# Keeping the third product's last tile on chip as the last stage's first tile, in a four-stage kernel on one core

## The chip, the core and the metric

The kernel runs on one core of a Trainium2 chip. The metric is the device time of one execution in microseconds (us). Three runs of the kernel before the change took 1687.85 to 1689.36 us, median 1688.62 us.

## What is computed

Attention in chunks of 64 over 8 batches of 8 heads, then a gated block (SwiGLU with a norm), then a block whose gate is `h * cos(h)`. Cut to what matters here:

```python
def _moe_ref(x, w_gate, w_val, w_out, rms_g):      # x: 4608 x 512, d_ff 1536
    ...
    return (silu * val @ w_out)

def _moe2_ref(x, w_in, w_out):                     # x: 4608 x 512, d_ff 2048
    h = x @ w_in
    g = h * np.cos(h)
    return (g @ w_out)
```

## The kernel before

Four stages follow each other, and TensorE (PE) does matmuls through all of them. Stage 1 does the attention and the two products with `w_gate` and `w_val`. Stage 2 multiplies by the first `w_out`. Stage 3 multiplies by `w_in` and applies the cosine gate. Stage 4 multiplies by the second `w_out` and stores the result. Stages 2 to 4 run over six tiles `s` of 768 tokens (`T`), each cut in two halves of 384 tokens (`H`, the block column `c`).

Each of these three products is made of 2 x 2 blocks `(r, c)` and of seven block products `j` in the place of eight: sums and differences of blocks are formed first (`operand`, `operand3`), then multiplied, and the seven results are combined. A block product `(s, j, g)`, called a product below, is 12 matmuls: two halves of the output by two chunks of the inner length by three, since every operand is split into a high and a low part. The high part is a cast on ScalarE (ACT) and the low part a subtraction on VectorE (DVE); both stand in `operand` (L249, L250) and every product needs both. The order of `j` is `PRODUCTS = (1, 7, 6, 2, 5, 4, 3)` in stage 4, with four groups `g` of features inside each `j`, so a tile is 28 products. In stage 4 product 1 needs the block (0, 0), product 7 the difference (1, 1) - (0, 1) in the buffer `tmp` (L235), product 6 two further differences (L238, L239), product 2 the block (1, 0), product 5 the changed (0, 1), product 4 another difference (L246), product 3 the block (1, 1). Operands are asked for `AHEAD = 5` products before their use. There is one buffer `tmp`.

Stage 3 ends every block with `turn`: for blocks (0, 0), (1, 1) and (0, 1) these are the sum `u` (L898, DVE), a cast to an integer (L906, ACT), a difference (L907, DVE), a sine (L908) and a square (L909, both ACT) and the last product (L910, DVE); block (1, 0) goes straight from PSUM through L912 (ACT), L913 and L914 (DVE), L915 (ACT) and L916 (DVE). The result stands in one of four buffers `r` and is stored to DRAM (`gd`, L919). In each group `g` the products 4 and 3 are put off into the next group (`tail`), so the last two products of stage 3 are 4 and 3 of group 3.

Stage 4 reads every block back from `gd`. For its first tile, tile 0, `early4` fetches a part of the blocks while stage 3 runs, for the six operands of `EARLY4`; the 14 other loads are issued at the start of stage 4 (L996 to L1003, issued through L820). Later tiles are fetched by `fetch4` once the products 4 and 3 have taken their operands of the tile ahead: two loads a group, each of both columns. All loads and stores stand in the one queue of SyncE (SP).

The weights of stage 4 (28 pieces of 512 KB, `w<-kout`, L158) take the places that stage 3's weights leave. The list `wanted` says which piece, or which early operand, takes the next place that `free` gives back. Five places are held back (`HELD`) to the start of stage 4.

The order of the instructions on PE is that of the code. That of ACT, DVE and SP in stages 3 and 4 is set by the framework's scheduler, which goes by its own estimate of when things are ready.

After the last matmul of the kernel, the last block is stored in two halves: one transposition (L981) and four stores each (L985).

Of the kernel before, what the change touches and what calls it, by code (L numbers as in the profile page):

```python
# [20 lines left out]
P = 128  # L21
# [11 lines left out]
SQ = 32  # L33
# [22 lines left out]
EARLY4 = 6  # L56
HELD = (2, 7, 5, 4, 3)
# [19 lines left out]
def kernel(  # L77
# [58 lines left out]
    wanted += last[:4] + [("op4", n, k) for n in range(EARLY4) for k in range(2)] + last[4:]  # L136
    place_of, weight, kept, early = {}, {}, {}, {}

    held = []

    def free(*tags):
        for tag in tags:
# [4 lines left out]
            if kind == "op4":  # L147
                continue
# [557 lines left out]
    made3 = [0]  # L706

    def fetch3(s):
        if s == 0:
            raw3[s] = {(r, c): early["x2", r, c] for r in range(2) for c in range(2)}  # L710
        elif s < NB:
            t = third_p.tile([P, 4, T], F32, tag="raw", name="rawx2", bufs=1)
            raw3[s] = blocks(t)
            c = s * T % PIECE
            nc.sync.dma_start(out=t, in_=x2d[s * T // PIECE][:, :, c : c + T])

    def operand3(s, j):
# [10 lines left out]
        pool = third_p if j in (1, 2, 6) else left_p  # L728
        o = pool.tile([P, 2, 2, H], F32R, tag="x3", name="x3", bufs=4)
        split(o, a, nc.vector)  # L730
# [79 lines left out]
    def fetch4(s, r, g):  # L810
        if s < NB:
            t = rw.tile([P, 2, T], F32, tag=f"raw{r}", name="rawg")
            raw4[s, g, r, 0], raw4[s, g, r, 1] = t[:, :, :H], t[:, :, H:]
            if s:
                load4(s, r, g, t, 0, T)
            return t

    def load4(s, r, g, t, lo, hi):
        c = s * T % PIECE
        nc.sync.dma_start(out=t[:, :, lo:hi], in_=gd[s * T // PIECE][:, g, 2 * r : 2 * r + 2, c + lo : c + hi])  # L820

    def operand4(s, j, g):
        n = made4[0]
        if n < EARLY4:
            tmp = third_p.tile([P, 2, H], F32, tag="tmp", name="tmp", bufs=1) if j == 7 else None
            to = [wp.tile([P, 2, H], F32R, tag=place_of["op4", n, k], name="xo") for k in range(2)]
            part = first4[g]
        else:
            tmp = tp.tile([P, 2, H], F32, tag="tmp", name="tmp") if j == 7 else None
            to = parts(xo_p)  # L830
            part = {(r, c): raw4[s, g, r, c] for r in range(2) for c in range(2)}
        ops4[s, j, g] = operand(j, part, tmp, lambda: to)
# [258 lines left out]
```

## Time and profile before

| | |
|---|---|
| runs, median (lowest to highest) | 1688.62 us (1687.85 to 1689.36) |
| profiled execution: its own time | 1687.49 us |
| profiled execution: span in the trace | 1685.7 us |
| PE busy | 1651.4 us, 98% |
| DVE busy | 1263.3 us, 75% |
| ACT busy | 860.2 us, 51% |
| HBM read, written | 183.24 MB, 125.30 MB |
| stage 4's first matmul | 1308.79 us |

The span runs from the first to the last instruction of the profiled execution; its own time is 1.79 us longer than that, for what lies around it. PE's busy time says little here, since matmuls are pipelined and their ends are modelled. What counts is how many matmuls go through in a stretch of time: in an undisturbed stretch all products take the same time, and a hold-up shows as fewer matmuls than that.

### The profile page before, as it was taken

To read this page: it belongs to the slowest core of one execution; us is meant where nothing else is said; L and a number is where in the kernel's file an instruction comes from. 1 tells how busy PE (TensorE), PEld (TensorE's weight loads), DVE (VectorE), ACT (ScalarE), POOL (GpSimd) and SP (SyncE) were. 2 spreads that over 40 slices of the span, in tenths; PEclk is the share of its full clock that TensorE was granted. 3 is DMA by queue.
4 is the path that set the end of the run, shared out by engine and by line. 5 is a ranking of instruction groups with operands and counts; after the bars stand their busy time and mean duration, and the time that the engine had idled before them with its cause. 6 is when DMAs were issued, how large, how long until landed. Compare 5 with 4: busy or idle time off the path is not lost.

```text
span 1685.7 us, 28029 instructions
## 1 busy us (share of the span) xinstructions
PE 1651.4 (98%) x11016; PEld 1535.1 (91%) x11016; DVE 1263.3 (75%) x1831; ACT 860.2 (51%) x1242; POOL 63.0 (4%) x104
## 2 busy tenths in 40 slices
PE   6999999999999999999999999999999899999998
PEld 5988888888888888999999999999999798999998
DVE  7974577787878741577777778888889668877885
ACT  4643344455444421344444488888888434434442
POOL 2321000000000000000000000000000000000000
PEclk9999999999999999999999999999999999999999
DMA  8523478788888828654445924324448962354331
GB/s 322 184 89 113 143 243 244 222 246 254 238 239 246 238 101 278 200 188 150 150 150 199 324 105 150 136 108 150 144 157 290 370 203 90 109 177 153 119 104 39
DMA packets 274661, 310.40 MB, mean 184 GB/s; under 512 B 83040, under 2 KB 218720, under 8 KB 274528
## 3 DMA queue, kind: packets, MB, share of 16 engines
q1 hardware_dynamic: 274528, 308.60, 55.7%
q8 instruction: 87, 1.43, 0.4%
q14 instruction: 46, 0.38, 0.1%
HBM read 183.24 MB, written 125.30 MB: 183 GB/s over the span
## 4 chain that ended last, share of the span: by engine, by line
PE 95%; DVE 3%; ACT 1%; DMA 1%; issue 1%; SPq 0%; POOL 0%; ACTq 0%; DVEq 0%
PE b L262 56%; PE v L262 18%; PE g L262 17%; PE o L453 1%; PE sc L359 1%; PE tr L429 1%; PE pt L397 1%; ACT xo L249 0%; DMA rawg<-gd 0%; DMA raw<-in_w_dram 0%; DVE rawg L239 0%; DVE xo L250 0%; DVE p L390 0%; DVE tmp L235 0%; DVE z L387 0%
## 5 line engine op out<-in xcount | busy, mean ns | idle before, releaser
L262 PE MATMUL b<-xo,w 128*128 128x384 f32 (+1 forms) x3576 | 621.6, 334 | 12.9 <-ACT xo L249 8.8
L262 PEld LDWEIGHTS b<-xo,w 128*128 128x128 f32 x3576 | 615.5, 188 | 18.9 <-ACT xo L249 12.0
L262 PE MATMUL b<-x,w 128*128 128x384 f32 x2016 | 351.8, 335 | 0.1
L262 PEld LDWEIGHTS b<-x,w 128*128 128x128 f32 x2016 | 349.0, 188 | 2.8 <-ACT z L893 2.1
L262 PE MATMUL v<-xt,w 128*128 128x512 f32 (+1 forms) x1416 | 321.7, 377 | 0.0
L262 PE MATMUL g<-xt,w 128*128 128x512 f32 (+1 forms) x1416 | 314.6, 372 | 0.0
L262 PEld LDWEIGHTS g<-xt,w 128*128 128x128 f32 x1416 | 250.0, 188 | 45.8
L262 PEld LDWEIGHTS v<-xt,w 128*128 128x128 f32 x1416 | 248.3, 190 | 44.9
L502 ACT ACTIVATE sg<-g 128x512 f32<-128x512 f32 (+1 forms) x118 | 66.1, 560 | 226.8 <-PE g L262 218.0
L249 ACT CAST xo<-rawg 128x768 fp32r<-128x768 f32 x140 | 114.8, 836 | 121.0 <-PE b L262 96.8
L250 DVE TENSOR_TENSOR xo<-rawg,xo 128x768 fp32r<-128x768 f32 x140 | 131.4, 953 | 51.6 <-ACT xo L249 51.3
L506 DVE TENSOR_TENSOR h<-sg,v 128x512 f32<-128x512 f32 (+1 forms) x100 | 67.5, 678 | 117.3 <-PE v L262 96.6
L249 ACT CAST xo<-rawh 128x768 fp32r<-128x768 f32 x102 | 81.6, 835 | 95.6 <-DMA rawh<-hd 49.2
L250 DVE TENSOR_TENSOR xo<-rawh,xo 128x768 fp32r<-128x768 f32 x102 | 93.0, 954 | 36.1 <-ACT xo L249 36.1
L910 DVE SCALAR_TENSOR_TENSOR r<-r,u 128x768 f32<-128x768 f32 x72 | 68.6, 953 | 21.5 <-ACT r L909 21.4
L908 ACT ACTIVATE r<-r 128x768 f32<-128x768 f32 x72 | 60.8, 845 | 33.3 <-DVE r L907 32.9
L907 DVE SCALAR_TENSOR_TENSOR r<-r,u 128x768 f32<-128x768 int32 x72 | 68.6, 953 | 11.1 <-ACT r L906 11.0
L898 DVE TENSOR_TENSOR u<-b,z 128x768 f32<-128x768 f32 x72 | 68.5, 952 | 7.9 <-ACT z L893 6.4
L249 ACT CAST xo<-tmp 128x768 fp32r<-128x768 f32 x42 | 35.2, 837 | 63.2 <-DVE tmp L235 62.6
L906 ACT CAST r<-u 128x768 int32<-128x768 f32 x72 | 59.7, 829 | 8.5 <-DVE u L898 8.5
L909 ACT ACTIVATE r<-r 128x768 f32<-128x768 f32 x72 | 60.9, 846 | 1.2
L893 ACT COPY z<-b 128x768 f32<-128x768 f32 x72 | 56.5, 793 | 7.1 <-PE b L262 5.2
(101 smaller groups left out, 1434.5 us busy)
## 6 DMA issues: line engine op xcount, KB each, us to landing
gd<-r SPq DMA_DIRECT2D x96, 384.0 KB, 2.5
rawg<-gd SPq DMA_DIRECT2D x42, 768.0 KB, 6.0
hd<-h SPq DMA_DIRECT2D x49, 512.0 KB, 4.6
kout<-wout SPq DMA_DIRECT2D x56, 448.0 KB, 4.7
w<-kout SPq DMA_DIRECT2D x49, 512.0 KB, 5.4
rawh<-hd SPq DMA_DIRECT2D x15, 1536.0 KB, 9.2
wraw<-in_w_dram SPq DMA_DIRECT2D x176, 128.0 KB, 3.2
qk<-in_qk_dram SPq DMA_DIRECT2D x36, 512.0 KB, 5.5
```

What stands on the lines that cost most here:

```text
L249: nc.scalar.copy(hi, a)
L250: nc.vector.tensor_tensor(lo, a, f32(hi), op=ALU.subtract)
L262: nc.tensor.matmul(acc, a, b, start=first and k == 0 and q == 0, stop=k == n - 1 and q == 2, skip_group_check=True)
L502: nc.scalar.activation(sg, g, AF.Silu)
L506: nc.vector.tensor_tensor(h, silu(acc[0]), acc[1], op=ALU.mult)
L893: nc.scalar.copy(t, acc)
L898: nc.vector.tensor_tensor(t, acc, part, op=ALU.add)
L906: nc.scalar.copy(k, u)
L907: nc.vector.scalar_tensor_tensor(q, k, -1.0, u, op0=ALU.mult, op1=ALU.add)
L908: nc.scalar.activation(q, q, AF.Sin, scale=math.pi)
L909: nc.scalar.activation(q, q, AF.Square, scale=math.sqrt(2 * PI2))
L910: nc.vector.scalar_tensor_tensor(q, q, -PI2, u, op0=ALU.add, op1=ALU.mult)
```

## The change

Stage 4 takes its tiles in the order 5, 0, 1, 2, 3, 4. `turn` leaves the 16 blocks of tile 5 in SBUF in the place of storing them: the blocks (0, c) in places of the weights (`z4` in `wanted`), the blocks (1, c) in tiles of their own (`quad`). Stage 4 uses them there as they are, and neither stores nor reads them. `early4`, `HELD` and the 14 loads at the start of stage 4 go. The places for early operands are now four pairs (`EARLY4 = 4`), for product 1 of tile 5.

Every block that is read back has a buffer of its own, named by its place (`q` + r, c, g): loads of 384 KB, one for each block, in the place of loads of 768 KB (stage 4) and of 1536 KB (stage 3's `fetch3`). Stage 3's ring of four result buffers becomes the four buffers of block (1, 1). A block is fetched as soon as its last reader is done: (0, 1) after product 5, (0, 0) and (1, 0) after product 4, (1, 1) after product 3. For tile 0 the blocks (0, c) are fetched at the end of stage 3.

Since 44 things now share 28 places, 16 of the 28 weight pieces of stage 4 come only when places get free in stage 4's first tile: 8 after its first four products, 4 after the operands of product 5, 4 after those of product 4.

The last transposition is cut in two (L984 to L986 of the changed kernel).

```diff
-EARLY4 = 6
-HELD = (2, 7, 5, 4, 3)
+EARLY4 = 4
...
-    wanted += last[:4] + [("op4", n, k) for n in range(EARLY4) for k in range(2)] + last[4:]
+    got = {c: [("z4", c, g) for g in range(4)] for c in range(2)}
+    op4 = [("op4", g, k) for g in range(EARLY4) for k in range(2)]
+    wanted += got[0][:1] + last[:4] + op4[:2] + got[1][:1] + got[0][1:2] + op4[2:4] + last[4:7]
+    wanted += got[1][1:2] + got[0][2:3] + op4[4:6] + last[7:10] + got[1][2:3] + op4[6:7] + got[0][3:]
+    wanted += op4[7:] + last[10:12] + got[1][3:] + last[12:]
...
+    def quad(r, c, k, dtype=F32):
+        pool = ring_p if (r, c) == (1, 1) else third_p
+        return pool.tile([P, 2, H], dtype, tag=f"q{r}{c}{k}", name="q")
...
-            t = third_p.tile([P, 4, T], F32, tag="raw", name="rawx2", bufs=1)
-            raw3[s] = blocks(t)
-            c = s * T % PIECE
-            nc.sync.dma_start(out=t, in_=x2d[s * T // PIECE][:, :, c : c + T])
+            raw3[s] = {(r, c): quad(1, 0, 2 * r + c) for r in range(2) for c in range(2)}
+            o = s * T % PIECE
+            for r in range(2):
+                for c in range(2):
+                    a = x2d[s * T // PIECE][:, 2 * r : 2 * r + 2, o + c * H : o + (c + 1) * H]
+                    nc.sync.dma_start(out=raw3[s][r, c], in_=a)
...
+    order4 = [NB - 1, *range(NB - 1)]
+    next4 = dict(zip(order4, order4[1:]))
+
+    def fetch4(s, r, c, g):
+        if s in next4:
+            s = next4[s]
+            raw4[s, g, r, c] = quad(r, c, g)
+            o = s * T % PIECE + c * H
+            nc.sync.dma_start(out=raw4[s, g, r, c], in_=gd[s * T // PIECE][:, g, 2 * r : 2 * r + 2, o : o + H])
 
     def operand4(s, j, g):
         n = made4[0]
+        tmp = third_p.tile([P, 2, H], F32, tag="tmp", name="tmp") if j == 7 else None
         if n < EARLY4:
-            tmp = third_p.tile([P, 2, H], F32, tag="tmp", name="tmp", bufs=1) if j == 7 else None
             to = [wp.tile([P, 2, H], F32R, tag=place_of["op4", n, k], name="xo") for k in range(2)]
-            part = first4[g]
         else:
-            tmp = tp.tile([P, 2, H], F32, tag="tmp", name="tmp") if j == 7 else None
             to = parts(xo_p)
-            part = {(r, c): raw4[s, g, r, c] for r in range(2) for c in range(2)}
...
+        ops4[s, j, g] = operand(j, {(r, c): raw4[s, g, r, c] for r in range(2) for c in range(2) if (s, g, r, c) in raw4}, tmp, lambda: to)
+        first = s == NB - 1
+        if j == 5:
+            if first:
+                free(place_of["z4", 1, g])
+            else:
+                fetch4(s, 0, 1, g)
+        elif j == 4:
+            if first:
+                free(place_of["z4", 0, g])
+            else:
+                fetch4(s, 0, 0, g)
+            fetch4(s, 1, 0, g)
+        elif j == 3:
+            fetch4(s, 1, 1, g)
...
+    seq4 = [(s, j, g) for s in order4 for j in PRODUCTS for g in range(G4)]
...
-            q = left_p.tile([P, 2, H], F32, tag="r", name="r", bufs=4)
+            if s < NB - 1:
+                k = ring[0] = (ring[0] + 1) % 4
+                q = quad(1, 1, k)
+            elif r == 0:
+                q = wp.tile([P, 2, H], F32, tag=place_of["z4", c, g], name="q")
+            else:
+                q = quad(1, c, g)
...
+            if s == NB - 1:
+                raw4[s, g, r, c] = q
+                return
...
+                if s == NB - 1 and g:
+                    ahead4(g)
...
-            nc.vector.transpose(o.rearrange("p t b j -> p b t j"), t.rearrange("p b (t j) -> p b t j", j=SQ))
+            if n < H:
+                for b in range(2):
+                    nc.vector.transpose(o[:, :, b], t[:, b].rearrange("p (t j) -> p t j", j=SQ))
+            else:
+                nc.vector.transpose(o.rearrange("p t b j -> p b t j"), t.rearrange("p b (t j) -> p b t j", j=SQ))
...
+        for c in range(2):
+            for g in range(G4):
+                fetch4(NB - 1, 0, c, g)
```

The change moves instructions on ACT and DVE. PE has the same matmuls in the same order.

On ACT, at the end of stage 3 and the start of stage 4, this stood before (L908 and L909 end the last `turn`; L989 copies the finished product 1 out of PSUM; `xo<-tmp` are the high parts for product 7, `xo<-rawg` those for products 6, 2, 5, 4, 3 and 1; the second number behind `b` tells the tile):

```order
L908 ACTIVATE r<-r 128x768
L909 ACTIVATE r<-r 128x768
L989 COPY s<-b_13148 128x768
L249 CAST xo<-tmp 128x768 x2
L249 CAST xo<-rawg 128x768 x8
L989 COPY s<-b_13148 128x768
L249 CAST xo<-rawg 128x768 x8
L989 COPY s<-b_13148 128x768
L249 CAST xo<-rawg 128x768 x8
L989 COPY s<-b_13650 128x768
L249 CAST xo<-tmp 128x768 x4
L249 CAST xo<-rawg 128x768 x8
```

and this now (L916 and L917 are the sine and the square, L920 and L923 belong to block (1, 0)):

```order
L920 ACTIVATE q<-b_12941 128x768
L250 CAST xo<-q 128x768
L916 ACTIVATE q<-q 128x768
L917 ACTIVATE q<-q 128x768
L923 ACTIVATE q<-q,halfpi 128x768
L914 CAST q<-u 128x768
L916 ACTIVATE q<-q 128x768
L917 ACTIVATE q<-q 128x768
L250 CAST xo<-tmp 128x768 x3
L996 COPY s<-b_13145 128x768
L250 CAST xo<-tmp 128x768
L250 CAST xo<-q 128x768 x8
```

The high part for product 1 of group 3 now stands inside the last turns, and three of the four casts for product 7 stand ahead of the copy, where before two of them had been made earlier and two stood behind it.

On ACT, where the second tile of stage 4 begins, this stands now (before: the row `L989 COPY s<-b_13650 128x768` above with all four casts for product 7 behind it):

```order
L250 CAST xo<-q 128x768 x8
L250 CAST xo<-tmp 128x768 x2
L996 COPY s<-b_13665 128x768
L250 CAST xo<-tmp 128x768 x2
L250 CAST xo<-q 128x768 x8
```

Two of the four casts for product 7 have moved ahead of the copy.

On DVE, at the end of stage 3, this stood before (L898 is the sum `u`, L907 and L910 belong to the turn of a whole block, L913, L914 and L916 to block (1, 0); L235, L238 and L239 are the differences for products 7 and 6, L250 the low parts):

```order
L913 SCALAR_TENSOR_TENSOR r<-r,b_12914 128x768
L914 TENSOR_SCALAR r<-r 128x768
L898 TENSOR_TENSOR u<-b_12976,z_12991 128x768
L910 SCALAR_TENSOR_TENSOR r<-r,u 128x768
L916 SCALAR_TENSOR_TENSOR r<-b_12914,r 128x768
L907 SCALAR_TENSOR_TENSOR r<-r,u 128x768
L910 SCALAR_TENSOR_TENSOR r<-r,u 128x768
L235 TENSOR_TENSOR tmp<-rawg 128x768
L250 TENSOR_TENSOR xo<-tmp,xo 128x768
L235 TENSOR_TENSOR tmp<-rawg 128x768
L250 TENSOR_TENSOR xo<-tmp,xo 128x768
L238 TENSOR_TENSOR rawg<-rawg 128x2x384
```

and this now (L900, L915, L918, L921, L922 and L924 are the turns, L236, L239 and L240 the differences, L251 the low parts):

```order
L921 SCALAR_TENSOR_TENSOR q<-q,b_12941 128x768
L251 TENSOR_TENSOR xo<-q,xo 128x768
L922 TENSOR_SCALAR q<-q 128x768
L918 SCALAR_TENSOR_TENSOR q<-q,u 128x768
L900 TENSOR_TENSOR u<-b_12999,z_13012 128x768
L924 SCALAR_TENSOR_TENSOR q<-b_12941,q 128x768
L915 SCALAR_TENSOR_TENSOR q<-q,u 128x768
L918 SCALAR_TENSOR_TENSOR q<-q,u 128x768
L251 TENSOR_TENSOR xo<-tmp,xo 128x768
L236 TENSOR_TENSOR tmp<-q 128x768
L239 TENSOR_TENSOR q<-q 128x768
L251 TENSOR_TENSOR xo<-tmp,xo 128x768
```

A low part (product 1, group 3) has come in among the last turns; the first difference for product 7 is made long before (it is not among these rows), its low part comes right behind the last turn, and the differences for product 6 are interleaved with those for product 7.

## Rows read from the trace of the kernel before

**Rows 1.** Windows: from:to, length, busy us of each engine (instructions), PE's clock, DMA share, GB/s.
```profile
1000.00:1300.00 300.00, 299.96 (x1723) 297.81 (x1722) 261.48 (x306) 253.12 (x328) 0.00 (x0) 1.00 0.44 155
...
1324.00:1326.00 2.00, 0.00 (x0) 0.00 (x0) 0.96 (x1) 0.62 (x1) 0.00 (x0) 0.50 1.07 397
...
1390.00:1400.00 10.00, 7.19 (x35) 5.46 (x33) 9.89 (x12) 3.29 (x5) 0.00 (x0) 1.00 0.01 2
```
**Rows 2.** Timeline of PE, stage 4's start: start, duration, count, [idle before, releaser].
```profile
1308.79 12.64 PE L262 MATMUL b<-xo,w 128*128 128x384 f32 x72
1326.26 0.69 PE L262 MATMUL b<-xo,w 128*128 128x384 f32 x1 [4.83 <-ACT xo L249]
...
1342.82 43.87 PE L262 MATMUL b<-xo,w 128*128 128x384 f32 x251 [0.16 <-ACT xo L249]
1388.31 0.45 PE L262 MATMUL b<-xo,w 128*128 128x384 f32 x1 [1.62 <-ACT xo L249]
...
1399.26 0.45 PE L262 MATMUL b<-xo,w 128*128 128x384 f32 x1 [0.47 <-ACT xo L249]
1399.99 50.30 PE L262 MATMUL b<-xo,w 128*128 128x384 f32 x288 [0.29 <-ACT xo L249]
```
**Rows 3.** Timeline of SP at the same place.
```profile
1306.75 0.37 SPq L919 DMA_DIRECT2D gd<-r  x1
...
1315.55 0.36 SPq L919 DMA_DIRECT2D gd<-r  x1
...
1317.37 12.44 SPq L820 DMA_DIRECT2D rawg<-gd  x14
```
**Rows 4.** Timeline of DVE: stage 3's end, stage 4's first two tiles.
```profile
1309.22 0.95 DVE L898 TENSOR_TENSOR u<-b,z 128x768 f32<-128x768 f32 x1
...
1314.56 0.96 DVE L910 SCALAR_TENSOR_TENSOR r<-r,u 128x768 f32<-128x768 f32 x1 [1.79 <-ACT r L909]
1324.38 0.96 DVE L235 TENSOR_TENSOR tmp<-rawg 128x768 f32<-128x768 f32 x1 [8.87 <-DMA rawg<-gd]
...
1388.29 0.96 DVE L250 TENSOR_TENSOR xo<-tmp,xo 128x768 fp32r<-128x768 f32 x1 [7.07 <-ACT xo L249]
1389.17 0.95 DVE L239 TENSOR_TENSOR rawg<-rawg 128x768 f32<-128x768 f32 x1
1390.03 0.95 DVE L235 TENSOR_TENSOR tmp<-rawg 128x768 f32<-128x768 f32 x1
```
**Rows 5.** Timeline of ACT: stage 3's end, stage 4's second tile.
```profile
1301.95 0.82 ACT L906 CAST r<-u 128x768 int32<-128x768 f32 x1
...
1306.90 0.81 ACT L912 ACTIVATE r<-b 128x768 int32<-128x768 f32 x1 [0.18 <-PE b L262]
...
1386.73 0.80 ACT L989 COPY s<-b 128x768 f32<-128x768 f32 x1 [9.57 <-PE b L262]
1387.42 0.83 ACT L249 CAST xo<-tmp 128x768 fp32r<-128x768 f32 x1
```
**Rows 6.** Timelines of DVE, then ACT, where the third tile begins.
```profile
1448.47 0.95 DVE L235 TENSOR_TENSOR tmp<-rawg 128x768 f32<-128x768 f32 x1
...
1452.24 0.80 ACT L989 COPY s<-b 128x768 f32<-128x768 f32 x1 [1.87 <-PE b L262]
```
**Rows 7.** Timeline of DVE: transpositions at the kernel's end; then PE's last half.
```profile
1670.48 0.98 DVE L981 STREAM_TRANSPOSE o<-s 128x768 f32<-128x768 f32 x1
1674.82 0.58 DVE L981 STREAM_TRANSPOSE o<-b 128x384 f32<-128x384 f32 x1 [3.37 <-PE b L262]
...
1675.46 5.60 PE L262 MATMUL b<-xo,w 128*128 128x192 f32 x48 [0.68 <-DVE o L981]
```
**Rows 8.** DMA issues, median us to landing: whole span, then 1300 to 1400 us.
```profile
gd<-r SPq DMA_DIRECT2D x96, 384.0 KB, 2.5
w<-kout SPq DMA_DIRECT2D x49, 512.0 KB, 5.4
...
w<-kout SPq DMA_DIRECT2D x18, 512.0 KB, 9.0
```

More of the change, by code (lines that the diff above doesn't have):

```diff
@@ L146, in free @@
             place_of[key] = tag
-            if kind == "op4":
+            if kind in ("op4", "z4"):
                 continue
@@ L719, in operand3 @@
         if j == 6:
-            raw3[s, "t"] = t = third_p.tile([P, 2, H], F32, tag="tmp", name="tmp", bufs=1)
+            raw3[s, "t"] = t = third_p.tile([P, 2, H], F32, tag="tmp", name="tmp")
             nc.vector.tensor_tensor(t, b[0, 1], b[0, 0], op=ALU.subtract)
@@ L727, in operand3 @@
         a = raw3[s, "t"] if j == 5 else b[{1: (0, 0), 2: (1, 0), 6: (0, 0), 7: (0, 1), 4: (1, 0), 3: (1, 1)}[j]]
-        pool = third_p if j in (1, 2, 6) else left_p
-        o = pool.tile([P, 2, 2, H], F32R, tag="x3", name="x3", bufs=4)
-        split(o, a, nc.vector)
+        if j in (1, 2, 6):
+            k = turn3[0] = (turn3[0] + 1) % 4
+            o = [quad(0, c, k, F32R) for c in range(2)]
+        else:
+            o = left_p.tile([P, 2, 2, H], F32R, tag="x3", name="x3", bufs=4)
+            o = [o[:, 0], o[:, 1]]
+        nc.scalar.copy(o[0], a)
+        nc.vector.tensor_tensor(o[1], a, f32(o[0]), op=ALU.subtract)
         ops3[s, j] = o
@@ L808 @@
     raw4, ops4 = {}, {}
[L810 to L820, printed above, removed]
+    order4 = [NB - 1, *range(NB - 1)]
@@ L877, in multiply @@
                     acc[:, p],
-                    [(w[:, e, 0, p], w[:, e, 1, p], x[:, 0, e], x[:, 1, e]) for e in range(2)],
+                    [(w[:, e, 0, p], w[:, e, 1, p], x[0][:, e], x[1][:, e]) for e in range(2)],
                     first,
@@ L881, in multiply @@
             if s == NB - 1:
-                held.append(place_of["in", g, PLACE_A[j]])
-                if not (g == G3 - 1 and j in HELD):
-                    free(held.pop())
+                free(place_of["in", g, PLACE_A[j]])
             if g == G3 - 1 and j != 1:
@@ L963 @@
     with ExitStack() as st:
-        rw = st.enter_context(tc.tile_pool(name="rw4", bufs=4, side="right", reuse_waits="tile"))
+        st.enter_context(third)
         xo_p = st.enter_context(tc.tile_pool(name="xo4", bufs=5, reuse_waits="tile"))
@@ L1013 @@
             xs[g] = take(n)
[L1014 removed]
+            if (s, j) == (order4[-1], PRODUCTS[-1]):
                 if g == G4 - 1:
```

45 lines of the change are left out of this document (4 added, 41 removed).

## The prediction

> **What bounds the kernel now.** I first read the windows for a stretch without trouble. In 300 us of stage 3 PE is busy for 299.96 us at a granted clock of 1.00 [rows 1], so stage 3 has no hole to fill, though DVE (261 us) and ACT (253 us) are nearly as full. Then I read PE's timeline where stage 4 begins, at 1308.79 us [rows 2]. An undisturbed run of 251 matmuls takes 43.87 us, 0.1748 us each, so a product of 12 takes 2.10 us and a tile of 28 takes 58.7 us. Against that pace two hold-ups stand out.
>
> The first: six products end at 1308.79 + 12.64 = 1321.43, and the undisturbed run starts at 1342.82. The program has 26 products (312 matmuls) from there to the end of that run, so 312 - 251 = 61 matmuls fell into these 21.39 us. They need 61 x 0.1748 = 10.66; **10.73 us are lost**. The row at 1326.26 names ACT's cast as what ended the 4.83 us of idling, but DVE's timeline shows the cause: the first difference for product 7 waited 8.87 us for a block from DRAM [rows 4], which SP had queued behind the last stores of stage 3 [rows 3]. In the idle stretch the granted clock fell to 0.50 (1.2 GHz) [rows 1], and this is part of the 10.73.
>
> The second: the run ends at 1342.82 + 43.87 = 1386.69, the next at full pace begins at 1399.99 [rows 2]. In these 13.30 us stand three products and one matmul (37 x 0.1748 = 6.47); **6.83 us are lost**. Here no load is late. ACT idles for 9.57 us in front of the copy of product 1, which waits for PE, and the casts for product 7 of the new tile stand behind that copy [rows 5]. DVE waits with them 7.07 us [rows 4]. Then the products follow each other every (1399.26 - 1388.31) / 3 = 3.65 us instead of 2.10 [rows 2], because DVE does four operations of 0.95 us for each (the two differences for product 6 stand between those for product 7). In this hold-up the granted clock stays 1.00 [rows 1].
>
> The third tile begins with the same pattern on DVE and loses nothing: the run at 1399.99 goes through. Its second difference starts at 1448.47, before the copy at 1452.24 that marks the end of product 1 [rows 6].
>
> **The change, part by part.** *Hold-up 1, the wait for DRAM.* Tile 5's blocks are on chip, so the 8.87 us wait goes, and with it the stores of 16 blocks of 384 KB and their loads. What is late next is the last turn: block (0, 1) of group 3 is needed for product 7 of group 3. More than that, the low part for product 7 of group 0 stands behind this turn on DVE, and its casts stand behind the turn's square on ACT (the rows of the order above). So the four-operation pattern starts when the last turn ends. How much this costs I read from how late DVE's second difference starts against the end of product 1, E. In hold-up 2 it starts at 1390.03, E + 3.34, and 6.83 us are lost [rows 2, 4]; in the third tile at 1448.47, 3.77 before the copy, and nothing is lost [rows 6]. Both agree with "lost = 3.5 + start against E" (3.5 - 3.77 is below nothing).
>
> Now the start in the changed kernel, with B for the first matmul of stage 4. Before, block (1, 0)'s cast starts at 1306.90, B - 1.89, the last sum at 1309.22, B + 0.43, and the last multiply at 1314.56, B + 5.77 [rows 4, 5]. Now ACT puts the cast for product 1 (0.83) behind the former, so sine and square of the second last turn end at B - 1.08 + 0.75 + 0.87 + 0.85 = B + 1.39 (an ACT operation that waits for nothing starts 0.69 to 0.75 after the one ahead, as the cast at 1387.42 does behind the copy [rows 5]), and DVE, in whose queue the sum now stands behind that turn's last step, starts the sum one step (0.87, as from 1388.29 to 1389.17 [rows 4]) later, at B + 2.28. From there the chain of six (sum, cast, difference, sine, square, multiply; 0.95 on DVE, 0.83 to 0.86 on ACT) puts the last multiply at B + 6.9, the first low part for product 7 at B + 7.75, and the second difference, which must wait for `tmp`, at B + 8.7. E is B + 8.39. So the start is E + 0.3 and **3.8 us are lost**. Bounds: if the added low part and cast delay nothing, the multiply ends the bare chain at B + 5.0, the start is E - 1.5 and 2.0 are lost; at the other end stands hold-up 2 itself, 6.83, with the same pattern started late.
>
> *Hold-up 2.* In the changed kernel two of the casts stand ahead of the copy at every tile after the first, as in the third tile before. Tile 0's blocks (0, c) are loaded a tile ahead, its (1, c) after products 4 and 3 of tile 5, some eight products (17 us) before their use, against 5.4 to 9.0 us for a piece that is even larger [rows 8]. All **6.83 us go**.
>
> *Weights.* Eight of the 28 pieces now wait for operands of stage 4's first tile. The operand of product 5, group 0, can be made when the fifth product ahead has let its buffer go, at B + 12 x 2.10 + 3.8 = B + 29; with 0.83 + 0.95 the place is free at B + 31; product 4 needs the piece at B + 20 x 2.10 + 3.8 = B + 46. That leaves 15 us for a load that lands in 5.4 (9.0 where the DMA is full) [rows 8]. Likewise for product 3. I cost this at nothing; the cover is 6 us.
>
> *Stage 3.* `fetch3` issues four loads for one, at some 0.4 us of SP each, beside 16 stores a tile: nothing while they don't hold stores up (a rival below). *The end.* A transposition of 768 columns takes 0.98 us and of 384 takes 0.58 [rows 7], so 192 take about 0.38 and two of them 0.68 with the overlap of neighbours on DVE (0.95 - 0.87): 0.1 more, 0.2 without overlap. PE waits for the first pair (the 0.68 idle row) as the stores wait for the second. Together **+0.2 us**, at most 0.4.
>
> *Sum.* 10.73 + 6.83 - 3.8 - 0.2 = 13.6 us saved. The profiled execution took 1687.49 (span 1685.7), so it becomes 1673.9; the median of the runs is 1.13 above it, hence **1675.1 us**.
>
> *The clock.* In hold-up 1 the clock fell in one idle stretch; in hold-up 2, with gaps up to 1.62 us [rows 2], it held at 1.00 [rows 1], and the new hold-up has gaps of hold-up 2's kind, so the sum takes full clock. The Trainium skill ("TensorE: Matmul & The Clock Gate", section "A second HAM failure mode: psum-queue depth-cycling") says that frequent short idling between groups of matmuls can also make the clock swing between half and full; by that rule the sum would be 1679.7 (second rival). Hold-up 2 speaks against the rule here.
>
> **The rivals.**
>
> *The second hold-up stays.* The order on ACT is better, but the wait could just pass to the blocks (1, c) of tile 0, whose loads stand in SP's queue behind weights and output stores. Then 6.83 come back: 1681.9. Against it speaks the 17 us of lead.
>
> *The clock halves in the new hold-up.* Four products at half clock take 4.2 us each, more than DVE's 3.65, so PE itself sets the pace: 4 x 2.1 = 8.4 lost for 3.8, 4.6 more, 1679.7. For it: such a fall is in this trace. Against: not in the stretch that resembles it.
>
> *The late weights bind.* If SP holds the eight loads back, product 4 or 3 waits. The gain is gone when the pieces come 13.6 us past the cover of 6, that is nearly 20 us late in all: no change, about 1688. The DMA is less loaded than before, which speaks against it.
>
> *Stage 3's stores get stuck behind its loads: slower.* There are now 16 single loads (four for each of tiles 2 to 5) among the stores in SP's queue, and each waits for the last reader of its own block. While one waits, finished blocks keep their four buffers. A buffer is held from the cast at 1301.95 to the store's issue at 1306.75 [rows 3, 5] and 2.5 until it lands [rows 8], 7.3 us; four buffers at 58.7 / 16 = 3.7 us a block give 14.7. So a load that waits up to 7.4 us at the head of the queue costs nothing; beyond that ACT, then DVE, then PE stand still. From 8.5 us of waiting on it is slower than before (16 x 1.1 = 17.6 against 13.6 saved): some 1692. For it: stage 3's engines have little slack to catch up. Against: the scheduler puts the loads between the stores at places of its own, and the single load of before cost PE nothing.
>
> **How the numbers follow.** My forecast has a chance of 0.77, with a range of its own from 1672.4 (2.0 lost at the new hold-up, less the spread of the runs, 0.8 either way) to 1679.0 (6.83 lost and 0.4 at the end). The clock has 0.07, the second hold-up 0.06, the weights 0.05, the stuck stores 0.05. A measurement of this kernel can tell some 0.2%, 3.4 us. The first three cases lie below 1685.2: faster 0.90; the weights about level, 0.05; slower 0.05. The range reaches from 1672 to 1682, over the clock and the second hold-up, and leaves out the last two.
>
> **What would show it.** PE's timeline after stage 4's first matmul: four products of product 1 at pace, then three steps near 3.65 us, some 3.8 us lost in all, releasers ACT and DVE and none a DMA; granted clock 1.00 throughout. DVE: no wait for a load near 1320. ACT: the copy at the second tile no longer with 9.57 us of idling, and no gap on PE there. In the DMA rows 80 stores to `gd` in the place of 96. Stage 4's first matmul near 1308.8 still; if it comes later, stage 3 has slowed and the fourth rival is at work. The prediction is wrong if PE's gaps in the first tile of stage 4 sum to more than 7 us, or one of them ends on a weight or a load.

## The result and the profile after

The changed kernel takes **1674.27 us** (median of 4 runs, 1672.56 to 1677.82), the kernel before 1688.99 (median of 4): ratio 0.9916, 95% interval 0.9899 to 0.9934. The profiled execution took 1674.01 us with a span of 1672.2, against 1687.49 and 1685.7: 13.5 us less span, where 13.6 were forecast. The forecast of the time was 1675.1 us, with a range from 1672 to 1682.

Windows of the changed kernel (columns as in [rows 1]), first the stretch of stage 3, then stage 4's start:

```profile
1000.00:1300.00 300.00, 300.00 (x1726) 298.51 (x1725) 259.98 (x303) 249.73 (x324) 0.00 (x0) 1.00 0.41 139
...
1310.00:1320.00 10.00, 9.88 (x58) 9.54 (x56) 8.10 (x11) 5.46 (x7) 0.00 (x0) 1.00 0.81 280
1320.00:1325.00 5.00, 3.53 (x17) 2.66 (x16) 4.97 (x6) 1.53 (x2) 0.00 (x0) 1.00 0.77 305
1325.00:1330.00 5.00, 4.03 (x22) 3.45 (x21) 4.97 (x7) 3.04 (x4) 0.00 (x0) 1.00 0.00 0
```

Stage 3 is as full as in [rows 1], and the granted clock, 0.50 there at 1324, stays 1.00. PE's timeline from stage 4's first matmul on, which answers to [rows 2]:

```profile
1309.15 11.14 PE L263 MATMUL b<-xo,w 128*128 128x384 f32 x61
1320.79 2.18 PE L263 MATMUL b<-xo,w 128*128 128x384 f32 x11 [0.49 <-DVE xo L251]
1323.39 0.45 PE L263 MATMUL b<-xo,w 128*128 128x384 f32 x1 [0.42 <-ACT xo L250]
1324.39 2.18 PE L263 MATMUL b<-xo,w 128*128 128x384 f32 x11 [0.55 <-DVE xo L251]
1326.99 0.45 PE L263 MATMUL b<-xo,w 128*128 128x384 f32 x1 [0.42 <-ACT xo L250]
1327.99 333.14 PE L263 MATMUL b<-xo,w 128*128 128x384 f32 x1931 [0.55 <-DVE xo L251]
1661.87 5.60 PE L263 MATMUL b<-xo,w 128*128 128x192 f32 x48 [0.74 <-DVE o L986]
```

From 1309.15 to 1327.99 there are 85 matmuls: 18.84 - 85 x 0.1748 = **3.98 us lost**, and nothing after them up to the last half product. Both hold-ups of [rows 2] are gone; the forecast new one is there, with steps of 3.60 us. On DVE (answers to [rows 4]):

```profile
1310.58 0.95 DVE L918 SCALAR_TENSOR_TENSOR q<-q,u 128x768 f32<-128x768 f32 x1
1311.44 0.95 DVE L900 TENSOR_TENSOR u<-b,z 128x768 f32<-128x768 f32 x1
...
1316.05 0.96 DVE L918 SCALAR_TENSOR_TENSOR q<-q,u 128x768 f32<-128x768 f32 x1 [1.79 <-ACT q L917]
1316.92 0.95 DVE L251 TENSOR_TENSOR xo<-tmp,xo 128x768 fp32r<-128x768 f32 x1
1317.91 0.96 DVE L236 TENSOR_TENSOR tmp<-q 128x768 f32<-128x768 f32 x1
...
1321.52 0.95 DVE L236 TENSOR_TENSOR tmp<-q 128x768 f32<-128x768 f32 x1
```

No wait for a load is left. SP, which answers to [rows 3], issues the last two of the next tile's loads and from then on weights only, each when its place comes free:

```profile
1300.90 0.87 SPq L830 DMA_DIRECT2D q<-gd  x2
1305.18 41.76 SPq L159 DMA_DIRECT2D w<-kout  x18
```

ACT at the second tile (answers to [rows 5]) has two casts ahead of the copy, whose idle time is 1.87 us where it was 9.57:

```profile
1373.73 0.84 ACT L250 CAST xo<-tmp 128x768 fp32r<-128x768 f32 x1 [3.18 <-DVE tmp L236]
1377.41 0.84 ACT L250 CAST xo<-tmp 128x768 fp32r<-128x768 f32 x1 [2.84 <-DVE tmp L236]
1380.12 0.80 ACT L996 COPY s<-b 128x768 f32<-128x768 f32 x1 [1.87 <-PE b L263]
1381.07 0.84 ACT L250 CAST xo<-tmp 128x768 fp32r<-128x768 f32 x1
```

At the kernel's end (answers to [rows 7]) the pair of transpositions on DVE takes 0.65 us where one took 0.58:

```profile
1661.16 0.65 DVE L986 STREAM_TRANSPOSE o<-b 128x192 f32<-128x192 f32 x2 [3.37 <-PE b L263]
```

The DMA issues (KB each, median us to landing) answer to [rows 8]: 80 stores in the place of 96.

```profile
gd<-q SPq DMA_DIRECT2D x80, 384.0 KB, 2.4
q<-gd SPq DMA_DIRECT2D x80, 384.0 KB, 4.1
...
w<-kout SPq DMA_DIRECT2D x49, 512.0 KB, 4.4
```

One wait is new, where stage 2 hands over to stage 3. PE's timeline, then ACT's:

```profile
956.86 4.33 PE L263 MATMUL b<-q,w 128*128 128x384 f32 x24
962.50 2.38 PE L263 MATMUL b<-q,w 128*128 128x384 f32 x12 [1.31 <-ACT z L895]
...
960.94 0.80 ACT L810 COPY x<-b 128x768 f32<-128x768 f32 x1 [3.05 <-DMA x2d<-x]
961.64 0.81 ACT L895 COPY z<-b 128x768 f32<-128x768 f32 x1
```

PE's third product here is product 6, which is added in PSUM on top of product 1, and so has to wait until ACT has copied product 1 to `z`. The kernel before shows no such wait, although its first copy to `z` comes later, 6.34 us after stage 3's first matmul and not 4.78:

```profile
957.07 351.87 PE L262 MATMUL b<-x,w 128*128 128x384 f32 x2016
...
963.41 0.80 ACT L893 COPY z<-b 128x768 f32<-128x768 f32 x1
```

Two products need 4.2 us, and PE goes through 2016 matmuls in one row, so there it can't have taken product 6 third. The description of the change has PE's matmuls in the same order in both kernels; at this place that is not so, and in the kernel before the order is not that of the code.

### The profile page after: what moved, and what is told of

Read it like the earlier page. It is cut to its first block, busy times and chain, and to the rows that moved or that the text cites. A ratio compares the mean times of both kernels' runs of the same rounds, so it can differ in the third digit from the quotient of the medians.

```text
span 1672.2 us, 28044 instructions
## 1 busy us (share of the span) xinstructions
PE 1646.9 (98%) x11016; PEld 1534.0 (92%) x11016; DVE 1264.7 (76%) x1833; ACT 859.1 (51%) x1242; POOL 63.2 (4%) x104
## 4 chain that ended last, share of the span: by engine, by line
PE 93%; DVE 3%; DMA 2%; ACT 1%; issue 0%; SPq 0%; POOL 0%; DVEq 0%; ACTq 0%
PE b L263 54%; PE v L263 18%; PE g L263 17%; PE o L454 1%; PE sc L360 1%; PE tr L430 1%; PE pt L398 1%; DMA raw<-in_w_dram 1%; DMA x2d<-x 0%; DMA q<-x2d 0%; DVE q L918 0%; DVE q L915 0%; DVE xo L251 0%; ACT q L916 0%; ACT q L917 0%
## 5 line engine op out<-in xcount | busy, mean ns | idle before, releaser
L263 PE MATMUL b<-x,w 128*128 128x384 f32 x1152 | 208.9, 335 | 0.0
L263 PEld LDWEIGHTS b<-x,w 128*128 128x128 f32 x1152 | 199.9, 188 | 1.6 <-ACT z L895 0.8
L250 ACT CAST xo<-q 128x768 fp32r<-128x768 f32 x144 | 118.1, 836 | 115.4 <-PE b L263 96.1
L251 DVE TENSOR_TENSOR xo<-q,xo 128x768 fp32r<-128x768 f32 x144 | 135.3, 954 | 53.3 <-ACT xo L250 53.1
L263 PE MATMUL b<-q,w 128*128 128x384 f32 x864 | 158.3, 334 | 1.3 <-ACT z L895 1.3
L263 PEld LDWEIGHTS b<-q,w 128*128 128x128 f32 x864 | 150.5, 188 | 1.6 <-ACT z L895 1.6
L250 ACT CAST xo<-rawh 128x768 fp32r<-128x768 f32 x102 | 81.6, 835 | 95.6 <-DMA rawh<-hd 49.1
L251 DVE TENSOR_TENSOR xo<-rawh,xo 128x768 fp32r<-128x768 f32 x102 | 93.0, 954 | 36.2 <-ACT xo L250 36.2
L918 DVE SCALAR_TENSOR_TENSOR q<-q,u 128x768 f32<-128x768 f32 x72 | 68.6, 953 | 18.9 <-ACT q L917 18.4
L900 DVE TENSOR_TENSOR u<-b,z 128x768 f32<-128x768 f32 x72 | 68.3, 952 | 17.3 <-ACT z L895 16.8
L915 DVE SCALAR_TENSOR_TENSOR q<-q,u 128x768 f32<-128x768 int32 x72 | 68.3, 953 | 12.7 <-ACT q L914 12.6
L916 ACT ACTIVATE q<-q 128x768 f32<-128x768 f32 x72 | 60.8, 844 | 30.9 <-DVE q L915 30.9
L250 ACT CAST xo<-tmp 128x768 fp32r<-128x768 f32 x42 | 35.2, 838 | 61.2 <-DVE tmp L236 60.5
L914 ACT CAST q<-u 128x768 int32<-128x768 f32 x72 | 59.7, 831 | 10.4 <-DVE u L900 10.3
```

The source lines that it names most:

```text
L250: nc.scalar.copy(hi, a)
L251: nc.vector.tensor_tensor(lo, a, f32(hi), op=ALU.subtract)
L263: nc.tensor.matmul(acc, a, b, start=first and k == 0 and q == 0, stop=k == n - 1 and q == 2, skip_group_check=True)
L900: nc.vector.tensor_tensor(t, acc, part, op=ALU.add)
L914: nc.scalar.copy(k, u)
L915: nc.vector.scalar_tensor_tensor(q, k, -1.0, u, op0=ALU.mult, op1=ALU.add)
```

## The experiments

The traces differ by up to 2.5 us in stage 1's start-up alone (PE's 64 matmuls from `pts` start between 433.06 and 435.58), so each trace is read from stage 4's first matmul (B) on: what is lost against 0.1748 us a matmul up to the undisturbed run (for the kernel before the prediction's 10.73; by this sum it is 10.78), and the time from B to the end of the span. E is B + 8.39, the end of product 1; "start" is VectorE's second difference for product 7 against E. By their times most of the variants can't be told from the changed kernel, since the intervals of the ratios overlap; what follows rests on one trace of each.

| run | median us | ratio to before, 95% | start | lost, first tile | B to the end |
|---|---|---|---|---|---|
| before | 1688.99 | | | 10.73 (+ 6.83 in the second) | 376.91 |
| changed | 1674.27 | 0.9899 to 0.9934 | +0.37 | 3.98 | 363.05 |
| changed again (a1) | 1673.86 | 0.9906 to 0.9935 | +0.38 | 3.98 | 363.09 |
| e1 | 1682.26 | 0.9953 to 0.9979 | | 11.63 | 371.82 |
| e2 | 1673.70 | 0.9895 to 0.9928 | -1.00 | 2.61 | 361.65 |
| e7 | 1676.99 | 0.9922 to 0.9951 | -1.01 | 2.85 (+ 3.19 in the second) | 365.61 |
| e11 | 1676.76 | 0.9925 to 0.9959 | +2.69 | 6.28 | 365.89 |
| e6 | 1679.74 | 0.9935 to 0.9965 | +2.17 | 5.52 (+ 3.19 in the second) | 368.00 |
| e8 | 1673.49 | 0.9899 to 0.9928 | -0.32 | 3.29 | 362.40 |
| e3 | 1673.96 | 0.9900 to 0.9930 | | 2.94 | 362.30 |
| e9 | 1672.12 | 0.9889 to 0.9922 | -1.00 | 1.99 | 361.21 |
| e10 | 1672.09 | 0.9899 to 0.9929 | -1.01 | 1.74 | 361.11 |
| e12 | 1671.45 | 0.9886 to 0.9919 | | 0.48 | 359.86 |
| e4 | 1673.69 | 0.9898 to 0.9928 | +0.39 | 3.99 | 363.10 |

> The changed kernel as it is, on the chip of the two other runs of this group: 1674.3 us, 4.0 us lost at the start of stage 4.

It repeats the changed kernel's trace from B on to 0.04 us.

**The second hold-up alone (e1).** The kernel before, with ACT in program order all through stage 4 (the loop stands one step further in):

```diff
-        for n, (s, j, g) in enumerate(seq4):
...
+        with tc.manual_schedule(engines={ET.Activation}):
+            for n, (s, j, g) in enumerate(seq4):
...
```

> The kernel before with one edit: in stage 4 ScalarE runs its copies and casts in program order, so the casts of product 7's four operands stand ahead of the copy of product 1 in every tile. Tile order, loads and buffers are those of before. Theory (the second hold-up of 6.83 us is made by the copy that waits for PE in front of the casts; the first, of 10.73 us, by the wait for DRAM): the gap at the second tile goes, the first stays, 1689.0 - 6.8 = 1682.2 us (1681 to 1684), and PE's run passes through the second tile. Rival (the second hold-up comes from loads that are late, or from VectorE's four operations for a product of 2.1 us, wherever the copy stands): both stay, 1688 to 1690 us.

PE's timeline of this run: the wait for DRAM stands, and one run, from 1344.46 to 1453.44, passes through the second tile's start.

```profile
1327.89 0.69 PE L262 MATMUL b<-xo,w 128*128 128x384 f32 x1 [5.67 <-ACT xo L249]
...
1344.46 108.98 PE L262 MATMUL b<-xo,w 128*128 128x384 f32 x624 [0.18 <-ACT xo L249]
```

From B on it is 5.09 us faster: 6.83 are gone, 0.90 more are lost in the first hold-up, and 0.63 in four new gaps of 0.15 or 0.16 in the later tiles, where now all four casts stand ahead of the copy; 0.2 are not assigned. The copy in front of the casts made the second hold-up.

**What removed the first hold-up (e2, e7, e11).** The three kernels start from the changed one.

e2: tile 5's row 1 is stored and read back; row 0 stays.

```diff
-            if s == NB - 1:
+            if s == NB - 1 and r == 0:
                 raw4[s, g, r, c] = q
                 return
...
+        for c in (1, 0):
+            for g in range(G4):
+                raw4[NB - 1, g, 1, c] = quad(1, c, g)
+                o = (NB - 1) * T % PIECE + c * H
+                a = gd[(NB - 1) * T // PIECE][:, g, 2:4, o : o + H]
+                nc.sync.dma_start(out=raw4[NB - 1, g, 1, c], in_=a)
```

> The changed kernel with one part undone: tile 5 is still stage 4's first tile, but its blocks (1, 0) and (1, 1), which the turns of row 1 make, are stored to DRAM and read back into the same kind of buffers when stage 4 begins; row 0 stays on chip. Theory (keeping the last tile on chip is what removed the first hold-up): product 7 waits for the read-back again, about 10 to 11 us are lost where the changed kernel loses 4.0, 1680 to 1682 us, with a stretch at a granted clock below 1.00. Rival (the order of the tiles and the buffers made the gain, the round trip itself is covered by product 1): 4 to 5 us lost, 1674 to 1675 us.

The rival came true: no PE wait on a load, and less lost than in the changed kernel, 2.61 us (the rival had 4 to 5). But row 1 is not what the last turn makes, so e7 sends everything:

```diff
             if s == NB - 1:
                 raw4[s, g, r, c] = q
-                return
...
+        for g in range(G4):
+            for r, c in ((0, 0), (1, 1), (0, 1), (1, 0)):
+                if r == 0:
+                    q = wp.tile([P, 2, H], F32, tag=place_of["z4", c, g], name="q")
+                else:
+                    q = quad(1, c, g)
+                raw4[NB - 1, g, r, c] = q
+                o = (NB - 1) * T % PIECE + c * H
+                nc.sync.dma_start(out=q, in_=gd[(NB - 1) * T // PIECE][:, g, 2 * r : 2 * r + 2, o : o + H])
```

> The changed kernel with all 16 blocks of tile 5 stored to DRAM and read back into their own buffers before product 7 uses them (product 1's operands, made earlier, still take the blocks on chip). The order of the tiles and the buffers stay. The run that sent only row 1 through DRAM lost nothing. Theory A (keeping the tile on chip is what removed the first hold-up): the last turn's block must go out and come back, 10 to 11 us lost at the start of stage 4 where the changed kernel loses 4.0, 1680 to 1682 us. Theory B (a buffer for every block, so that each load starts as soon as its block is stored, is what removed it; the trip itself is covered): the last block comes back at about 6.9 + 0.95 + 0.4 + 2.4 + 0.4 + 4.1 = 15 us after stage 4's first matmul, just before VectorE reaches it, 4 to 6 us lost, 1674 to 1676 us.

Theory B in kind, though in neither number: 2.85 us are lost at the start and not 4 to 6, and the time lies 1 us above its 1674 to 1676. DVE waits for a load once, for the last group, by 0.16 us:

```profile
1323.42 0.96 DVE L236 TENSOR_TENSOR tmp<-q 128x768 f32<-128x768 f32 x1 [0.16 <-DMA q<-gd]
```

The start is earlier than in the changed kernel because the scheduler put the last sum earlier on DVE, not because of DRAM. From B on the run is 2.56 us slower than the changed kernel: it loses 3.19 in the second tile, where this program has one cast ahead of the copy (below). e11 keeps the buffers and turns the order of the tiles back:

```diff
-    order4 = [NB - 1, *range(NB - 1)]
+    order4 = [*range(NB)]
...
+        def first4(r, c, g):
             if r == 0:
                 q = wp.tile([P, 2, H], F32, tag=place_of["z4", c, g], name="q")
             else:
                 q = quad(1, c, g)
+            raw4[0, g, r, c] = q
+            nc.sync.dma_start(out=q, in_=gd[0][:, g, 2 * r : 2 * r + 2, c * H : (c + 1) * H])
...
+            if s == NB - 1 and (r, c) != (1, 1):
+                first4(r, c, g)
...
-            if s == NB - 1:
-                raw4[s, g, r, c] = q
-                return
...
+        for g in range(G4):
+            first4(1, 1, g)
...
```

> The changed kernel with stage 4's tiles in the order of before, tile 0 first and tile 5 last: all of tile 5's blocks go to DRAM, tile 0's come from it into the 16 buffers in which the changed kernel leaves tile 5 (the four blocks (1, 1) when the last turns have let go of theirs). Product 7 does not need the last turn now, but the last of the (1, 1) loads lands about 14.5 us after stage 4's first matmul. Theory B (a buffer of its own for every block, filled while stage 3 runs, removed the first hold-up): 2 to 5 us lost, 1672 to 1676 us. Theory A (the tile that stays on chip removed it): the loads beside stage 3's last stores bring the wait back, 8 to 11 us lost, 1678 to 1682 us.

6.28 us are lost, 1.28 above theory B's range and 1.72 under theory A's, and the time of 1676.76 lies between the two as well, nearer to B; the clock is 1.00. The first difference for product 7 waits 0.57 us for its load, and the four-operation pattern starts late, at E + 2.69:

```profile
1316.58 0.96 DVE L236 TENSOR_TENSOR tmp<-q 128x768 f32<-128x768 f32 x1 [0.57 <-DMA q<-gd]
```

So of the 6.75 us by which the first hold-up shrank, 4.45 (10.73 to 6.28) came with the rest of the change, above all the buffers, which let loads run beside stage 3, and 2.30 (to 3.98) with tile 5 first. That the tile stays on chip is not needed for either: e7 sends it out and back, and loses, but for 0.36 us, what its start makes it lose (product 1's operands alone still come from the blocks on chip). That it was the buffers, and not another of the things in which e11 still differs from the kernel before, as the places of the weights, is argued, not tried.

**The law of the loss (e6, e8, e3).** e6 makes the last turn's chain longer:

```diff
                 nc.vector.scalar_tensor_tensor(q, k, -1.0, u, op0=ALU.mult, op1=ALU.add)
+                for _ in range(3 if (s, g, r, c) == (NB - 1, N2 // 4 - 1, 0, 1) else 0):
+                    nc.vector.tensor_scalar(q, q, -4.0, 4.0, op0=ALU.max, op1=ALU.min)
```

> The changed kernel with three clamps added on VectorE (which change no value) in the last turn of stage 3, between its difference and its sine: about 3 x 0.87 = 2.6 us more ahead of the last multiply. Theory (what is lost is 3.5 us plus the start of VectorE's second difference against the end of product 1): 4.0 + 2.6 = 6.6 us lost at the start of stage 4, 1676.9 us. In this program the scheduler puts one cast, not two, ahead of the copy of product 1 in the second tile; by the same rule that stays free or costs under 0.5 us. Rival (the loss is set by ScalarE's casts or by PE's own start, VectorE has slack): still 4.0 us, 1674.3 us.

The three clamps take 1.75 us, not 2.6: an operation with one source is cheaper here than the two-source ones that I took the price from (one alone takes 0.55 us, a two-source one 0.95). The start is E + 2.17, so the law gives 5.67 us; measured 5.52. The rest of the run's lag is in the second tile, where I expected under 0.5 us. ACT there:

```profile
1377.32 0.84 ACT L250 CAST xo<-tmp 128x768 fp32r<-128x768 f32 x1 [3.18 <-DVE tmp L236]
1383.70 0.80 ACT L998 COPY s<-b 128x768 f32<-128x768 f32 x1 [5.55 <-PE b L263]
1384.40 0.84 ACT L250 CAST xo<-tmp 128x768 fp32r<-128x768 f32 x1
```

Between 1385.93 and 1393.32, where PE's undisturbed runs end and begin, lie 24 matmuls: one cast ahead of the copy costs 7.39 - 24 x 0.1748 = 3.19 us, in e7 as here. None ahead costs 6.83 [rows 2, 5], two nothing, and four (e1, e9, e10, e12) at most 0.16.

e8 makes the last chain earlier, by taking product 3 and its turn ahead of product 4 in the last group:

```diff
-    wanted += op4[7:] + last[10:12] + got[1][3:] + last[12:]
+    wanted += op4[7:] + last[10:11] + got[1][3:] + last[11:]
...
+            swap = s == NB - 1 and g == G3 - 1
+            if swap:
+                multiply(z["b5"], s, 3, g, False)
+                turn(total(z["b5"], z16), s, g, 0, 1, True)
             multiply(z["b1"], s, 4, g, False)
             turn(z["b1"], s, g, 1, 0, False)
+            if swap:
+                return
```

> The changed kernel with the last two products of stage 3's last group swapped, product 3 with its turn of block (0, 1) first, product 4 with its turn of block (1, 0) last (one buffer is claimed one weight earlier for it). Product 7 needs (0, 1), and (1, 0) is not needed before product 2. Theory (lost = 3.5 us plus the start of VectorE's second difference against the end of product 1): the sum can start up to 2.1 us earlier, the second difference about 2 us ahead of the end of product 1, 1 to 2 us lost instead of 4.0, 1671.5 to 1672.5 us. Rival (VectorE has a debt of work at this place, so that an earlier start of one chain only delays another): 3 to 4 us lost, 1673.5 to 1674.5 us.

The scheduler let other turn steps in between, the start moved by only 0.69 us to E - 0.32, and 3.29 us are lost (law: 3.18). Loss and time are those of the rival: VectorE had other work due at this place. The law of the loss held, my forecast of the start did not.

e3 takes tile 5's products in the order 1, 2, 7, 6, 5, 4, 3 (the kernel's own is 1, 7, 6, 2, 5, 4, 3):

```diff
+SEQ5 = (1, 2, 7, 6, 5, 4, 3)
...
-    last = [("out2", g, PLACE_A[j]) for j in PRODUCTS for g in range(N2 // 4)]
+    last = [("out2", g, PLACE_A[j]) for j in SEQ5 for g in range(N2 // 4)]
...
-    seq4 = [(s, j, g) for s in order4 for j in PRODUCTS for g in range(G4)]
+    seq4 = [(s, j, g) for s in order4 for j in (SEQ5 if s == NB - 1 else PRODUCTS) for g in range(G4)]
```

> The changed kernel with the products of tile 5 in stage 4 taken in the order 1, 2, 7, 6, 5, 4, 3 (1, 7, 6, 5, 2, 4, 3 or the like before), their weights in that order too. Product 2 needs one VectorE operation for an operand, product 7 three or four. Theory (the 4.0 us that the changed kernel still loses at the start of stage 4 come from VectorE's and ScalarE's preparation of product 7 behind the last turn): product 2's 8.4 us cover it, 0.5 to 2 us lost instead of 4.0, 1670.5 to 1672.5 us. Rival (the loss lies in the passage between the stages, whatever the product): 4 us lost, 1674.3 us.

PE's timeline: no wait is listed behind product 1, but two come later. 2.94 us are lost in all, 0.64 of them in small gaps among the 133 matmuls ahead of the first row.

```profile
1335.81 10.50 PE L264 MATMUL b<-xo,w 128*128 128x384 f32 x59 [1.22 <-DVE xo L252]
1347.20 113.04 PE L264 MATMUL b<-xo,w 128*128 128x384 f32 x647 [0.89 <-ACT s L997]
```

DVE is busy without a gap from 1317.59 to 1346.17. Product 2 covers product 7's first operands, but DVE's backlog is only put off: my 0.5 to 2 us left out that the differences for products 7, 6 and 5 all follow.

**Its pace (e9, e10, e12).** In e9 DVE's order for products 7 and 6 of the first tile is written out, with product 6's second differences behind product 7; in the second tile ACT runs in program order. (`between` issues product 6's first difference while ACT casts.)

```diff
         nc.scalar.copy(hi, a)
+        if between:
+            between()
         nc.vector.tensor_tensor(lo, a, f32(hi), op=ALU.subtract)
...
+        start.enter_context(tc.manual_schedule(engines={ET.DVE}))
...
```

> The changed kernel with VectorE's order written out for products 7 and 6 of stage 4's first tile: the first difference for product 6 stands under the cast of product 7, the second one after the last operand of product 7, so product 7 costs VectorE three operations a group (2.7 us) instead of four (3.6 us). In the second tile ScalarE's four casts for product 7 stand ahead of the copy. The scheduler also moves the last turns a little, as in the run with row 1 through DRAM, where 2.6 us were lost. Theory (the 3.5 us are the four-operation pattern, 3 x (3.6 - 2.1) and less): 0.5 to 1.5 us lost at the start of stage 4, 1671 to 1672 us. Rival (the start of the pattern alone counts, not its pace): 2.6 us lost, 1672.8 us.

1.99 us are lost with the start at E - 1.00, where the four-operation law gives 2.50: less than the rival's 2.6, more than the 0.5 to 1.5 that I expected. The steps are 2.86 us (1316.68, 1319.54, 1322.39). Most of what is left is one wait of 1.36 us on PE, for the last operand of product 7, ahead of which I had put a difference for product 6 (L847):

```profile
1324.26 0.95 DVE L847 TENSOR_TENSOR q<-q 128x768 f32<-128x768 f32 x1
1325.13 0.95 DVE L254 TENSOR_TENSOR xo<-tmp,xo 128x768 fp32r<-128x768 f32 x1
```

e10 puts it behind, and adds the edit of e4 (below).

> The run with the differences after product 7, with two edits: the first of product 6's second differences stands behind the last operand of product 7 (it stood ahead of it, where PE waited 1.36 us), and tile 1's loads for stage 3 are issued where stage 3 begins. Theory (each wait is where it was read): 2.0 - 0.9 = 1.1 us lost at the start of stage 4 and a wait of 0.5 us at stage 3, 1670.5 us; 3.8 under the changed kernel. Rival (another order of VectorE only moves the wait to product 6): 2 us lost, 1671.5 us.

1.74 us, not 1.1, and 1672.09 us, not 1670.5: part of the wait moved to product 6, which is nearer to the rival's 2 us.

e12 takes the single `tmp` away, whose reuse made each difference wait for the operand ahead; product 7's differences go to the four buffers that tile 0's blocks (0, 1) fill later.

```diff
+        def seven(k):
+            tmps[k] = quad(0, 1, k)
+            sub(k, tmps[k], (1, 1), (0, 1))
...
+        if first and j == 7:
+            fetch4(s, 0, 1, g)
```

> The changed kernel with VectorE's order for products 7 and 6 of stage 4's first tile written out once more: product 7's four differences get a buffer each (those that tile 0's blocks (0, 1) fill afterwards), so that they no longer wait for one another, and product 6's differences stand behind them. Product 7 then costs VectorE two operations a group behind the last turn, 1.75 us against PE's 2.10. Theory (lost = the start against the end of product 1, plus three times what the pace of VectorE exceeds PE's 2.10 us): no wait in product 7, 0.2 to 0.8 us lost at the passage to product 6, 1670.5 to 1671 us. Rival (VectorE's whole work after the last turn sets the loss, in whatever order): as with three operations, 1.7 to 2.0 us, 1672 us.

PE's timeline: 133 matmuls without a gap, then 0.45 us in the last group of product 6.

```profile
1310.54 23.28 PE L267 MATMUL b<-xo,w 128*128 128x384 f32 x133
1334.27 50.22 PE L267 MATMUL b<-xo,w 128*128 128x384 f32 x288 [0.45 <-DVE xo L255]
```

It loses 0.48 us, as the theory had it and not the rival, and is 3.2 us shorter from B on than the changed kernel. Its median of 1671.45 us lies 0.45 above the range expected. The intervals of its ratio and of the changed kernel's overlap, so by times alone e12 and the changed kernel are not told apart; it is the trace that shows the gain.

**The new wait at stage 3 (e4).** One group of loads is moved:

```diff
                     fetch3(0)
-                    fetch3(1)
                     ahead3(3)
...
+        fetch3(1)
         ahead3(7)
```

> The changed kernel with one of stage 3's loads of four blocks (tile 1's) issued where stage 3 begins instead of at the end of stage 2. Theory (the new wait of 1.3 us on PE at the beginning of stage 3 comes from these loads, which share the DMA with the stores that free ScalarE's copy buffers): the wait falls under 0.3 us, 1673.0 us. Rival (the copies wait for other traffic, the weights above all): it stays at 1.3 us, 1674.3 us; and if tile 1's blocks now come late, PE waits for them a tile later.

The wait is 0.52 us in e4, but 1.24 in e10 with the same edit, and between 0.64 and 1.51 in the runs without it. ACT's copy does start sooner (956.63 and 957.75, 960.94 in the changed kernel), but the scheduler then puts it, and the wait for its buffer's store, ahead of four casts. So the fall under 0.3 us that I expected did not come, and with runs without the edit down to 0.64 it is not shown that the loads have a part at all. What the profile after does show is that PE's order changed here: in the kernel before the copy to `z` came even later and PE did not need it yet. No run here turns that order back, so what the wait would be without it stays open.

## Why the prediction was right

*The new hold-up, 3.8 us: 3.98.* Step by step the replay held: last sum at B + 2.28 (seen 2.29), last multiply B + 6.9 (6.90), first low part B + 7.75 (7.77), second difference B + 8.7 (8.76). One step of it came out by luck: I let the last sum wait for the square on ACT, but in the trace DVE has no wait between 1307.51 and that sum. DVE's own work set its start; the step ahead of it (1310.58) came only 0.15 us after the square's end. The law "lost = 3.5 + start against E", read from two places of one trace, held at six starts from -1.01 to +2.69 with errors of 0.36 us at most (0.15 without e7). Only one of the two places had fixed the 3.5, hold-up 2; the other, with nothing lost, merely did not speak against it. The 3.5 can be counted, too: in the changed kernel 10.08 us pass from the second difference (1317.91) to the last matmul that waits (1327.99), and PE at pace needs 37 x 0.1748 = 6.47 for the matmuls from E to there, which leaves 3.61. e9 to e12 show that it is the four-operation pace. With three operations less is lost than the law says, with two nothing in product 7.

*Hold-up 2, 6.83 us: all gone*, by the step named: casts ahead of the copy. e1 shows it alone. The Trainium skill ("PSUM — Partial Sum Buffer", section "Engine vs sequencer instructions") states that ScalarE's queue is strictly first in, first out; the trace agrees, since in the kernel before the first cast's data was ready at 1380.23 (the difference for product 7 on DVE) and the cast began only behind the copy, at 1387.42. What I had not seen is how easily the scheduler undoes it: two edits elsewhere left one cast ahead and cost 3.19 us.

*Hold-up 1, 10.73 us: gone, but for a reason that I put too narrowly.* I wrote that the wait goes because tile 5's blocks are on chip. e7 shows that the round trip of the same tile through DRAM is hidden but for 0.36 us at most, and e11 that 4.45 of the 6.75 us come without the new order of the tiles. That the buffers do it is the likely reading, not a shown one.

*Weights and stage 3 at nothing.* No gap in 1931 matmuls speaks for the first. Stage 3's inside is full, but its beginning has the new wait of 1.31 us: I took PE's order for unchanged, and it was not. From a common point in stage 1 (PE's product with `pts`, at 434.07 and 433.86) to B it is 874.72 before and 875.29 now: 0.57 us that I did not have. That is less than the wait; where in stage 3 the other 0.74 came back was not followed up.

*The end, +0.2 us: 0.13* (0.65 for 0.58 on DVE, 0.74 for 0.68 on PE). I had put the pair at 0.68.

*The sum.* 10.73 + 6.83 - 3.98 - 0.13 = 13.45; B to the end shrank by 13.86. The 0.4 left is not assigned. That the span shrank by 13.5, so near to the 13.6, is partly luck: these 0.4 and a start-up shorter by 0.21 (434.07 to 433.86) happen to make up for the 0.57 in stage 3.

*The rivals.* The second hold-up and late weights did not come; stores stuck behind loads neither (PE 300.00 of 300 in stage 3). The clock stayed at 1.00 in the changed kernel, with gaps of 0.42 to 0.55 us, and so did not do what is said of frequent short idling in the Trainium skill ("TensorE: Matmul & The Clock Gate", section "A second HAM failure mode: psum-queue depth-cycling").

## What to carry to other kernels

A round trip through memory that looks like the cause of a wait may only lack buffers (here the likely reading): send the same data through once more with the new buffers, before paying for keeping it on chip. Where an in-order engine both empties PE's results and prepares PE's operands, count how many preparations stand ahead of each emptying, after every edit. A hold-up at a stage boundary is the start of the preparing chain plus its pace against PE's, and the pace can be cut by moving work that belongs to later products behind.

## What was not expected of the hardware

In e6 the granted clock did fall to 0.50 (1.2 GHz), after idling of 0.96 and 0.70 us with one matmul between. Windows of that run:

```profile
1318.00:1320.00 2.00, 1.58 (x10) 1.26 (x8) 0.21 (x2) 1.92 (x3) 0.00 (x0) 1.00 1.12 389
1320.00:1322.00 2.00, 0.76 (x2) 0.51 (x3) 1.97 (x3) 0.49 (x1) 0.00 (x0) 0.95 0.89 336
1322.00:1324.00 2.00, 2.00 (x7) 2.00 (x7) 1.97 (x3) 1.34 (x2) 0.00 (x0) 0.50 0.99 387
1324.00:1326.00 2.00, 2.00 (x10) 2.00 (x10) 2.00 (x3) 0.19 (x1) 0.00 (x0) 0.70 0.88 358
```

In e11 idling of 0.86 and 0.56 us in the same place left it at 1.00. Of the runs here, then, e6 alone fits what the Trainium skill says of frequent short idling in the section named above, and its clock fell once. It cost e6 nothing that the loss shows: 24 matmuls took 6.02 us in the place of 4.20, but DVE, at 3.6 us a group, was slower still, and the loss of 5.52 us lies under the 5.67 that the law gives at full clock. In the prediction's rival the half clock was to cost 4.6 us, because four whole products were put at 1.2 GHz; here two were, and in part.
